# Interleaved attention layers on one core: local scores and values as two tasks each, the band tile kept in SBUF and loaded as rectangles, new orders

## The chip, the cores and the metric

One core of one Trainium2 chip runs the whole program in one launch. The metric is the device time of an execution in microseconds (us). A core has five engines with queues of their own: TensorE (PE; its weight loads are listed as PEld), VectorE (DVE), ScalarE (ACT), GpSimd (POOL) and SyncE (SP), which issues nearly all DMA transfers here. Each engine works its queue off in order.

## The reference

Four layers follow each other, of kinds A, B, A, B, each on the layer norm of its input, with a residual sum. Sequence 2048, width 512, 32 heads of 16, float32.

```python
def _A_ref(x, wqkv, wo):                 # dilated window: 8 keys, 2 apart
    W, dil = 8, 2
    idx = pos[:, None] - off[None, :]    # off = arange(W) * dil
    logits = einsum("bhsd,bhswd->bhsw", q, kg) * Dh ** -0.5   # kg, vg: k, v at idx
    attn = softmax(where(idx >= 0, logits, -1e9))
    return reshape(einsum("bhsw,bhswd->bhsd", attn, vg)) @ wo

def _B_ref(x, wqkv, wo):                 # the last 256 keys
    mask = (i - j >= 0) & (i - j < 256)
    p = softmax(where(mask, einsum("bhqd,bhkd->bhqk", q, k) * Dh ** -0.5, -1e9))
    return reshape(einsum("bhqk,bhkd->bhqd", p, v)) @ wo

x = A_x
for f, w in ((_A_ref, A), (_B_ref, B), (_A_ref, A), (_B_ref, B)):
    x = x + f(_layernorm(x), *w)
```

## The kernel before

The sequence is cut into 8 chunks of 256 positions. For each pair of layers (A, B) and each chunk, `layer_a` and then `layer_b` add their steps as tasks to a planner, 16 such pairs in all. A task has an engine, an estimated duration, the values that it reads and writes, and a place. The places stand in the table `ORDER`, one number for each task: each engine's queue is sorted by them, so that the table alone fixes the order on an engine. `Plan.order` then plays the queues through with its estimates, and thereby chooses PSUM banks and the sequence in which the instructions are written.

The projections (`proj_t`, lines 1013 to 1015, and `proj_n`, lines 1033 to 1036) are large matmuls of 256 or 512 columns in three float16 products. The rest of TensorE's work are small matmuls on parts of the array. In layer A, a chunk is split into even and odd positions, t = 0 and 1, of 128 positions each:

- `scores` (line 1159), 64 matmuls for each t, gives each block of 32 queries its 39 keys (`WIN`); a trip through DRAM (`shelve`, `band`) picks the 8 of each query; then comes the softmax.
- The softmax's weights are written into `bands`. `put` (line 1244) stores them in a zeroed DRAM buffer `ptd` with a stride that shifts each query's 8 weights to the right place among 39 keys, and `get` (line 1250) loads the result as the band tile `pt`: 39 partitions (keys), for 2 x 16 pairs of queries and 32 heads, in two transfers, one for each half of the partitions. `window` (line 1239) loads the values `vs` of the same keys.
- `mix` (line 1267), 64 matmuls for each t, multiplies the two; `pick` follows on VectorE, then `finish` with the output projection.

The float32 matmuls of `scores`, `mix` and of the values of layer B run as two passes each, so a task of 64 matmuls is 256 instructions of TensorE with its weight loads. The pool of `pt` has one buffer, so the second `get` of a chunk waits for the first `mix`.

In layer B, line 1377 (q) computes scores for the row maxima, which VectorE takes (lines 1396 and 1392); lines 1528 and 1583 are the scores and values themselves, between them ScalarE's exponentials (1538, 1550) and masks on GpSimd or VectorE (1567, 1561). Its queries and keys come as stk<-re (line 1319), the row maxima through md (1428, 1434). Line 1709 are matmuls on nothing that keep TensorE busy early in the program; there are 110 such tasks.

Of the kernel before, what the change touches and what calls it, by code (L numbers as in the profile page):

```python
# [11 lines left out]
F32 = mybir.dt.float32  # L12
# [6 lines left out]
P = 128  # L19
# [415 lines left out]
SLOW = 0.25  # L435
LEAVE = {"Q": 0.13, "C": 0.185, "X": 0.15, "V": 0.17, "R": 0.13, "F": 0.105, "": 0.0}
AGAIN = {"PE": 0.0, "DVE": 0.11, "ACT": 0.12, "POOL": 0.055, "SP": 0.0}
RECENT, WARM, EDGE = 3.4, 0.31, 0.05


class Buf:
# [206 lines left out]
def kernel(  # L648
# [276 lines left out]
    def norm(l, c):  # L925
# [31 lines left out]
        for t in range(2):  # L957
            if layers[l] == "A" and (l, c) != (0, 0):
# [8 lines left out]
                def low(xn=xn):  # L967
                    return xn.t.bitcast(F16)[:, 0:D]
# [780 lines left out]
```

## Time and profile before

| | |
|---|---|
| time, median of 3 runs | 1544.56 us (1534.9 to 1547.74) |
| the profiled execution | 1535.14 us, span of its instructions 1533.4 us |
| mean granted TensorE clock | 0.937 |
| TensorE busy | 1352.3 us |
| VectorE, ScalarE, GpSimd busy | 869.0, 829.8, 386.9 us |
| DMA | 203.06 MB, mean 132 GB/s |

Busy time is the time in which an engine has an instruction under way, and small matmuls run beside each other. Idle time is listed with what ended it: "issue" is a wait for nothing that the profile shows. A profile line such as "L1267 <- DMA pt<-ptd" reads: the instruction of line 1267 waited for the transfer from `ptd` to `pt`.

### The profile page before, as it was taken

The page shows a single profiled execution, that of the slowest core. Times are in us where ns is not written, and L with a number is a line of the kernel's source. Part 1 is how long each engine was busy: PE and PEld are TensorE (multiplying, and loading weights), DVE is VectorE, ACT ScalarE, POOL GpSimd, SP SyncE. Part 2 cuts the span into 40 slices and gives each one's busy share as a digit, 9 for nine tenths or more (in the row PEclk, how much of TensorE's full clock was granted, in tenths as well). Part 3 has the DMA queues.
Part 4 walks back from the last instruction along what each step waited for, and adds up shares of the span by engine and source line. Part 5 has one row for each costly group of instructions (what it writes and reads, how often), then busy time and mean ns, then how long its engine had stood idle before and what let it go on. Part 6 is the DMA issues. An engine that isn't in the chain of part 4 may idle for free.

```text
span 1533.4 us, 64202 instructions
## 1 busy us (share of the span) xinstructions
PE 1352.3 (88%) x28126; PEld 870.6 (57%) x28126; DVE 869.0 (57%) x1966; ACT 829.8 (54%) x1301; POOL 386.9 (25%) x828
## 2 busy tenths in 40 slices
PE   8989989898898988979889897989989899897876
PEld 7665657465464745646456463755647375564643
DVE  5635664754636455455663617466562755646486
ACT  8634647465654655636555373647657355453633
POOL 3410202222213323213132031315033311231231
PEclk9999999889999999999899898999999999898988
DMA  9874463645537255553445647365464646536222
GB/s 252 217 170 138 129 129 109 152 118 150 120 108 168 81 166 112 143 143 106 113 98 167 129 133 162 85 171 127 140 123 125 149 101 155 121 105 158 81 80 58
DMA packets 183377, 203.06 MB, mean 132 GB/s; under 512 B 92188, under 2 KB 122652, under 8 KB 183096
## 3 DMA queue, kind: packets, MB, share of 16 engines
q1 hardware_dynamic: 182840, 198.69, 51.2%
q8 instruction: 220, 3.60, 1.0%
q14 instruction: 61, 0.50, 0.1%
q10 hardware_dynamic: 256, 0.26, 0.1%
HBM read 101.97 MB, written 79.36 MB: 118 GB/s over the span
## 4 chain that ended last, share of the span: by engine, by line
PE 55%; DMA 16%; DVE 10%; issue 7%; SPq 7%; ACT 5%; POOL 1%; DVEq 0%; ACTq 0%; POOLq 0%
PE banks L1583 7%; PE banks L1013 7%; PE banks L1014 6%; PE banks L1015 6%; PE banks L1033 4%; PE banks L1035 4%; DMA pt<-ptd 4%; PE banks L1377 4%; PE banks L1036 4%; PE banks L1528 4%; PE banks L1267 3%; DVE m L1392 3%; PE banks L1159 2%; DMA sd<-s 2%; SPq L1308 2%
## 5 line engine op out<-in xcount | busy, mean ns | idle before, releaser
L1392 DVE TENSOR_REDUCE m<-banks 128x2 f32<-128x512 f32 x448 | 302.6, 689 | 9.0
L1538 ACT ACTIVATE p<-banks,sclB 128x896 f32<-128x896 f32 x224 | 221.3, 1006 | 77.4 <-PE banks L1528 62.1
L1396 DVE COPY_PREDICATED banks<-trm,banks 128x128 f32<-128x128 int16 x448 | 125.4, 291 | 150.6 <-PE banks L1377 142.6
L1377 PE MATMUL banks<-stk,stk 48*64 48x192 f16 (+3 forms) x3584 | 147.8, 249 | 49.1 <-DMA stk<-re 15.7
L1567 POOL TENSOR_SCALAR_AFFINE_SELECT p<-p 64x256 f32<-64x256 f32 x296 | 116.7, 416 | 271.4 <-ACT p L1538 258.9
L1567 POOL TENSOR_SCALAR_AFFINE_SELECT ps<-ps 64x256 f32<-64x256 f32 x272 | 109.3, 423 | 255.9 <-ACT ps L1550 251.1
L1377 PEld LDWEIGHTS <-stk 48*64 48x64 f16 x3584 | 83.0, 111 | 141.8 <-issue 117.3
L1528 PE MATMUL banks<-stk,stk 64*64 64x128 f16 (+3 forms) x3584 | 126.8, 245 | 22.8 <-ACT p L1538 7.7
L1583 PE MATMUL banks<-p,v 64*32 64x192 f32 (+1 forms) x3584 | 129.9, 386 | 9.6 <-issue 6.0
L1550 ACT ACTIVATE ps<-banks,sclB 128x768 f32<-128x768 f32 x112 | 100.1, 899 | 50.5 <-PE banks L1528 36.1
L1528 PEld LDWEIGHTS <-stk 64*64 64x64 f16 x3584 | 71.8, 110 | 84.6 <-issue 73.0
L1167 ACT COPY s<-banks 128x624 f32<-128x624 f32 x64 | 74.5, 1263 | 60.2 <-DMA sd<-s 32.6
L1298 DVE SCALAR_TENSOR_TENSOR el<-banks,eh 128x512 f16<-128x512 f32 x64 | 42.8, 688 | 106.0 <-ACT eh L1295 79.8
L1267 PE MATMUL banks<-pt,vs 39*32 39x64 f32 x4096 | 63.1, 252 | 37.9 <-DMA pt<-ptd 18.4
L1583 PEld LDWEIGHTS banks<-p,v 64*32 64x32 f32 x3584 | 68.6, 113 | 46.7 <-issue 24.0
L1600 ACT COPY os<-banks 128x256 f32<-128x256 f32 x112 | 41.3, 373 | 95.7 <-PE banks L1583 91.1
L1597 DVE TENSOR_TENSOR os<-os,banks 128x256 f32<-128x256 f32 x104 | 42.7, 418 | 87.9 <-ACT os L1600 79.8
L1583 PE MATMUL banks<-ps,v 64*32 64x64 f32 (+1 forms) x3584 | 77.0, 260 | 12.2 <-issue 12.1
L1583 PEld LDWEIGHTS banks<-ps,v 64*32 64x32 f32 x3584 | 69.1, 112 | 22.5 <-issue 18.4
L1267 PEld LDWEIGHTS banks<-pt,vs 39*32 39x32 f32 x4096 | 52.5, 114 | 51.3 <-issue 33.2
L1014 PE MATMUL banks<-xl,wA0h 128*128 128x256 f16 x256 | 71.9, 281 | 1.7 <-issue 1.7
L1013 PE MATMUL banks<-xh,wA1h 128*128 128x256 f16 x256 | 70.8, 277 | 2.7 <-DMA xh<-ht 2.7
(214 smaller groups left out, 3107.4 us busy)
## 6 DMA issues: line engine op xcount, KB each, us to landing
stk<-re SPq DMA_DIRECT2D x256, 96.0 KB
sd<-s SPq DMA_DIRECT2D x128, 156.0 KB
pt<-ptd SPq DMA_DIRECT2D x64, 312.0 KB
re<-eh SPq DMA_DIRECT2D x128, 128.0 KB
vs<-vd SPq DMA_DIRECT2D x64, 156.0 KB
vd<-ve SPq DMA_DIRECT2D x32, 256.0 KB
xm<-y SPq DMA_DIRECT2D x32, 256.0 KB
re<-el SPq DMA_DIRECT2D x64, 128.0 KB
```

The source lines that it names most:

```text
L1013: nc.tensor.matmul(ps[mp].t[:, i], wh, xh, start=k == 0, stop=False)
L1014: nc.tensor.matmul(ps[mp].t[:, i], wh, xl, start=False, stop=False)
L1015: nc.tensor.matmul(ps[mp].t[:, i], wl, xh, start=False, stop=k == 3)
L1267: nc.tensor.matmul(acc.t[32 * r : 32 * r + 32, bb].rearrange("p (a x q u) -> p a x q u", a=2, q=16, u=2)[:, :, 2 * m + b2], vs.t[k, b2, 32 ...
L1377: nc.tensor.matmul(o, lhs, k, start=True, stop=True, tile_position=(64 * par, 64 * h))
L1392: nc.vector.tensor_reduce(out=m.t[:, :, u, qb], in_=ps.t[:, :, 0 : 2 * P], op=ALU.max, axis=AX.X)
L1396: nc.vector.copy_predicated(t[:, :, 0:64], trm[:, 0].bitcast(I16).unsqueeze(1).broadcast_to([P, 2, 64]), t[:, :, C : C + 64])
L1528: nc.tensor.matmul(ps.t[64 * h : 64 * h + 64, par, at + x0 : at + x0 + q1 - q0], stk[hf, kt][r, col, k0 : k0 + 64], stk[hf, 0][r, col, q0: ...
L1538: nc.scalar.activation(big.t[:, 2 * i : 2 * i + 2], ps.t[:, :, 0:448], AF.Exp, scale=scl["B", 1])
L1550: nc.scalar.activation(small.t.rearrange("p (i m) x -> p m i x", i=2), ps.t[:, :, 0:384].rearrange("p m (i x) -> p m i x", i=2), AF.Exp, s ...
L1567: E.affine_select(out=v, in_=v, pattern=[[0, 4], [a, 64]], compare_op=op, fill=0.0, base=0, channel_multiplier=-a)
L1583: nc.tensor.matmul(acc.t[32 * mm : 32 * mm + 32, h, q0:q1], vv[r, blk, 17 * hd : 17 * hd + 32], x.t[r, mm, x0 : x0 + q1 - q0], start=begin ...
```

## The change

1. The band tile becomes one constant tile `ptt`, zeroed once on GpSimd. `get` loads, for each half of the partitions, two rectangles in place of the whole: for the first 8 pairs of queries the first 23 keys, for the last 8 pairs the last 23 keys. What lies outside stays zero. There are four transfers of 23 partitions for each `get` in place of two of 39.
2. `scores` and `mix` become two tasks each, of half the matmuls, so that other work can stand between the halves.
3. The planner has a new term: TensorE's instructions are fetched at `FETCH` each us into a store of `STORE`, each task says how many it takes (`rec`), and a task can't be shorter than its instructions take to come.
4. Some estimates change: size 1350 of `get` becomes 700, its time on SyncE 0.8 becomes 1.65; sizes of `clear`, the transposes and `shelve`, and the time of the masks on GpSimd grow.
5. The table `ORDER` is new throughout, one list for each scope.

```diff
 ORDER = {
-    "S": [16, 13, 12, 0, 11, 7, 6, 35, 19],
+    "S": [13, 21, 3, 19, 0, 2, 7, 20, 21, 13],
...
+FETCH, STORE = 67.0, 160.0
...
-                us /= clock
+                store = min(STORE, store + FETCH * (now - seen))
+                us = max(us / clock, (t.rec - store) / FETCH)
+                store = min(STORE, store + FETCH * us - t.rec)
+                seen = now + us
...
+    ptt = cst.tile([P, 2, 16, H, 2], F32, name="ptt")
+    vptt = Val()
...
+    plan.add("POOL", 1.8, lambda: nc.gpsimd.memset(ptt, 0.0), w=[vptt])
...
-            def scores(t=t, pbs=pbs):
-                for m in range(4):
+            def scores(m0, t=t, pbs=pbs):
+                for m in range(m0, m0 + 2):
...
-            plan.add("PE", 1.5, scores, r=[*vq, *vk, vhalo], w=vpb, mode="X", act=0.7)
+            for m0 in (0, 2):
+                plan.add("PE", 0.75, lambda f=scores, m0=m0: f(m0), r=[*vq, *vk, vhalo], w=vpb, mode="X", act=0.35, rec=128)
...
-            def get(t=t, pt=pt):
+            def get(t=t):
                 x = ptd[t]
                 for bb in range(2):
-                    nc.sync.dma_start(pt.t[64 * bb : 64 * bb + WIN].rearrange("p a q s u -> p a (q s u)"),
-                                      bass.AP(tensor=x.tensor, offset=x.offset + 2 * bb * 65 * H * 32, ap=[[64 * H, WIN], [65 * H * 32, 2], [1, 32 * H]]))
+                    for e in range(2):
+                        nc.sync.dma_start(ptt[64 * bb + 16 * e : 64 * bb + 16 * e + WIN - 16, :, 8 * e : 8 * e + 8].rearrange("p a q s u -> p a (q s u)"),
+                                          bass.AP(tensor=x.tensor, offset=x.offset + (2 * bb * 65 * 32 + 16 * e * 65) * H, ap=[[64 * H, WIN - 16], [65 * H * 32, 2], [1, 16 * H]]))
...
-            plan.add("SP", 0.8, get, r=[vptd[t]], w=[vpt], size=1350)
+            plan.add("SP", 1.65, get, r=[vptd[t]], w=[vptt], size=700)
...
-            def mix(acc=acc, vs=vs, pt=pt):
-                for m in range(4):
+            def mix(m0, acc=acc, vs=vs):
+                for m in range(m0, m0 + 2):
...
-            plan.add("PE", 2.0, mix, r=[vvs, vpt], w=[va], mode="V", act=1.2)
+            for m0 in (0, 2):
+                plan.add("PE", 0.85, lambda f=mix, m0=m0: f(m0), r=[vvs, vptt], w=[va], mode="V", act=0.5, rec=128)
```

Lines of the changed program lie 12 to 14 further down than before (`mix` at 1280, `scores` at 1171, `get` at 1263). Three places of the order:

SyncE, chunk 4 of the first pair of layers, from the first `get` to past the second (md, stk: layer B's row maxima, queries and keys; xl, xh, y, x: inputs; vs: local values). Before:

```order
L1250 DMA pt_4_0_6424<-ptd_148 39x2x1024 x2
L978 DMA_TRANSPOSE xl_5_6390<-xn_5_0_5363 128x4x128
L1428 DMA md_3_0_6453<-mt_3_0_6427 4x32x32 x2
L977 DMA_TRANSPOSE xh_5_6325<-ht_5_0_5385 128x4x128
L1099 DMA y_4_0_6505<-in_A_x_dram 128x512
L1434 DMA stk_0_132<-md_3_0_6453 2x1024 x2
L1250 DMA pt_4_1_6600<-ptd_149 39x2x1024 x2
L1428 DMA md_3_1_6612<-mt_3_1_6510 4x32x32 x2
```

And now:

```order
L1263 DMA ptt<-ptd_146 23x2x512 x4
L1442 DMA md_3_0_6492<-mt_3_0_6465 4x32x32 x2
L1333 DMA stk_2_134<-re_3_1_5640 48x1x1024 x2
L1256 DMA ptd_147<-bands 64x9x64
L1448 DMA stk_0_129<-md_3_0_6492 2x1024 x2
L1251 DMA vs_4_1_6636<-vd_1_149 39x2x512 x2
L1263 DMA ptt<-ptd_147 23x2x512 x4
L1442 DMA md_3_1_6727<-mt_3_1_6704 4x32x32 x2
```

Each `get` is four transfers with 23 rows in place of two with 39, and other transfers stand behind it.

TensorE, the `mix` of chunk 4 in the second pair of layers, t = 0. Before, behind layer B's values:

```order
L1583 MATMUL banks<-ps_3_1_19846,v_140 32x64
L1583 MATMUL banks<-ps_3_1_19846,v_138 32x64
L1267 MATMUL banks<-pt_4_0_19861,vs_4_0_19622 32x2x32 x64
L1013 LDWEIGHTS wA0h
L1013 MATMUL banks<-xh_5_19885,wA0h 128x256
L1014 LDWEIGHTS wA0h
```

And now:

```order
L1391 LDWEIGHTS stk_0_132
L1391 MATMUL banks<-stk_2_134,stk_0_132 64x128
L1280 MATMUL banks<-ptt,vs_4_0_19498 32x2x32 x64
L1025 LDWEIGHTS wA0h
L1025 MATMUL banks<-xh_5_19761,wA0h 128x256
L1026 LDWEIGHTS wA0h
```

The values of layer B have gone from in front of the `mix`; its two halves still follow each other, as one row of 64.

TensorE, the two `scores` of the first chunk. Before they are one run:

```order
L1709 LDWEIGHTS idf
L1709 MATMUL banks<-idf 128x256
L1159 MATMUL banks<-k_0_270,qm_0_483 64x39 x128
L1013 LDWEIGHTS wA1h
L1013 MATMUL banks<-xh_1_456,wA1h 128x256
```

And now the first of them, the second coming some 80 rows later:

```order
L862 MATMUL banks<-idf,axA_540 2x128
L1171 MATMUL banks<-k_0_489,qm_0_474 64x39 x64
L881 MATMUL banks<-a1A_588,ones 128x4
L1723 LDWEIGHTS idf
L1723 MATMUL banks<-idf 128x256
```

The run of 128 matmuls has become two of 64.

More of the change, by code (lines that the diff above doesn't have):

```diff
@@ L497 @@
 class Task:
-    __slots__ = ("eng", "us", "fn", "n", "after", "bufs", "mode", "start", "end", "size", "act", "place", "ready", "scope", "alt")
+    __slots__ = ("eng", "us", "fn", "n", "after", "bufs", "mode", "start", "end", "size", "act", "place", "ready", "scope", "alt", "rec")
 class Plan:
@@ L507, in begin, with add @@
         self.scope, self.k = scope, 0
-    def add(self, eng, us, fn, r=(), w=(), mode="", size=0, act=0.0, alt=None):
+    def add(self, eng, us, fn, r=(), w=(), mode="", size=0, act=0.0, alt=None, rec=5):
         t = Task()
-        t.eng, t.us, t.fn, t.mode, t.size, t.act, t.scope = eng, us, fn, mode, size, act, self.scope
+        t.eng, t.us, t.fn, t.mode, t.size, t.act, t.scope, t.rec = eng, us, fn, mode, size, act, self.scope, rec
         t.place, t.alt = ORDER[self.scope][self.k] if self.scope in ORDER else len(self.tasks), alt
@@ L556, in order @@
         dma, mode, tail, use, since = 0.0, "", "", 0.0, 0.0
+        store, seen = STORE, 0.0
         out = []
@@ L673 @@
     cst = ctx.enter_context(tc.tile_pool(name="cst", bufs=1))
-    for name, bufs in (("px", 4), ("pqm", 1), ("pk", 1), ("psc", 1), ("pl", 1), ("ppt", 1), ("pvs", 1), ("pve", 1), ("po4", 1), ("pos", 2), ("pxn", 2),
+    for name, bufs in (("px", 4), ("pqm", 1), ("pk", 1), ("psc", 1), ("pl", 1), ("pvs", 1), ("pve", 1), ("po4", 1), ("pos", 2), ("pxn", 2),
                        ("pxt", 2), ("pp6", 2), ("pp7", 2), ("pqk", 2), ("poh", 2), ("ps1", 1), ("psm", 2)):
@@ L771 @@
     for i in range(2):
-        plan.add("SP", 1.5, lambda i=i: clear(i), r=[vbands], w=[vptd[i], vvd[0, i, -1], vvd[2, i, -1]], size=1100)
+        plan.add("SP", 1.5, lambda i=i: clear(i), r=[vbands], w=[vptd[i], vvd[0, i, -1], vvd[2, i, -1]], size=1500)
     wt, vwt, psc, pscs, scl, vscl = {}, {}, {}, {}, {}, {}
@@ L976, in norm @@
                 plan.add("POOL", 1.12, rest, r=[vxn, vht], w=[vlt], mode="S", alt=("DVE", 0.6))
-                plan.add("SP", 1.24, lambda sl=sl, ht=ht: nc.sync.dma_start_transpose(xh.t[:, :, sl], ht.t), r=[vht], w=[vh], size=16)
-                plan.add("SP", 1.24, lambda sl=sl, low=low: nc.sync.dma_start_transpose(xl.t[:, :, sl], low()), r=[vlt], w=[vl], size=16)
+                plan.add("SP", 1.28, lambda sl=sl, ht=ht: nc.sync.dma_start_transpose(xh.t[:, :, sl], ht.t), r=[vht], w=[vh], size=200)
+                plan.add("SP", 1.28, lambda sl=sl, low=low: nc.sync.dma_start_transpose(xl.t[:, :, sl], low()), r=[vlt], w=[vl], size=200)
                 continue
@@ L1181, in band @@
                                   bass.AP(tensor=x.tensor, offset=x.offset, ap=[[2 * (WIN + 1) * H, 64], [(WIN + 1) * H, 2], [1, W * H]]))
-            plan.add("SP", 1.9, shelve, r=vS, w=[vsd], size=450)
+            plan.add("SP", 1.9, shelve, r=vS, w=[vsd], size=600)
             plan.add("SP", 0.4, band, r=[vsd], w=[vL[t]], size=160)
@@ L1232, in layer_a @@
             vs = buf("pvs", [P, 2, D], F32, "vs", f"vs{l}_{c}_{t}")
-            pt = buf("ppt", [P, 2, 16, H, 2], F32, "pt", f"pt{l}_{c}_{t}")
-            vvs, vpt = Val(vs), Val(pt)
+            vvs = Val(vs)
             def window(t=t, vs=vs):
@@ L1267, in mix @@
                                 nc.tensor.matmul(acc.t[32 * r : 32 * r + 32, bb].rearrange("p (a x q u) -> p a x q u", a=2, q=16, u=2)[:, :, 2 * m + b2],
-                                                 vs.t[k, b2, 32 * (4 * m + r) : 32 * (4 * m + r) + 32], pt.t[k, :, :, 16 * b2 + 4 * m + r],
+                                                 vs.t[k, b2, 32 * (4 * m + r) : 32 * (4 * m + r) + 32], ptt[k, :, :, 16 * b2 + 4 * m + r],
                                                  start=True, stop=True, tile_position=(64 * bb, 32 * r))
@@ L1379, in layer_b @@
                     if first:
-                        plan.add("PE", 0.172, scores, r=[vst[hf, 0, hp], vst[hf, now, hp]], w=[vps], mode="R", act=0.14)
+                        plan.add("PE", 0.172, scores, r=[vst[hf, 0, hp], vst[hf, now, hp]], w=[vps], mode="R", act=0.14, rec=8)
                     else:
-                        plan.add("PE", 0.15, halves, r=[vst[hf, 0, hp], vst[hf, now, hp], vst[hf, bef, hp]], w=[vps], mode="Q", act=0.12)
+                        plan.add("PE", 0.15, halves, r=[vst[hf, 0, hp], vst[hf, now, hp], vst[hf, bef, hp]], w=[vps], mode="Q", act=0.12, rec=16)
                     def top(u=u, qb=qb, ps=ps, m=m, x0=x0):
@@ L1476, in expo @@
                                                      AF.Exp, scale=scl["B", 1])
-                            plan.add("PE", 0.172, scores, r=[vst[hf, 0, hp], vst[hf, "m", hp], vst[hf, kt, hp]], w=[vps], mode="R", act=0.14)
+                            plan.add("PE", 0.172, scores, r=[vst[hf, 0, hp], vst[hf, "m", hp], vst[hf, kt, hp]], w=[vps], mode="R", act=0.14, rec=8)
                             plan.add("ACT", 0.8, expo, r=[vps, vscl["B", 1]], w=[vp[i]])
@@ L1503, in layer_b @@
                         nxt = Val(acc)
-                        plan.add("PE", 0.67, values, r=[vp2, *vvt[(c - 1 + b) % 3], *([chain] if chain else [])], w=[vacc, nxt], mode="C", act=0.16)
+                        plan.add("PE", 0.67, values, r=[vp2, *vvt[(c - 1 + b) % 3], *([chain] if chain else [])], w=[vacc, nxt], mode="C", act=0.16, rec=64)
                         chain = nxt
@@ L1538, in expo @@
                         nc.scalar.activation(big.t[:, 2 * i : 2 * i + 2], ps.t[:, :, 0:448], AF.Exp, scale=scl["B", 1])
-                    plan.add("PE", 0.205, lambda f=score, ps=ps, i=i: f(ps, 0, i, wide_), r=need, w=[vps], mode="Q", act=0.165)
+                    plan.add("PE", 0.205, lambda f=score, ps=ps, i=i: f(ps, 0, i, wide_), r=need, w=[vps], mode="Q", act=0.165, rec=16)
                     plan.add("ACT", 0.93, expo, r=[vps, vscl["B", 1]], w=[vbig[i]])
@@ L1551, in expo @@
                                          AF.Exp, scale=scl["B", 1])
-                plan.add("PE", 0.18, thin, r=need, w=[vps], mode="Q", act=0.14)
+                plan.add("PE", 0.18, thin, r=need, w=[vps], mode="Q", act=0.14, rec=32)
                 plan.add("ACT", 0.8, expo, r=[vps, vscl["B", 1]], w=[vsmall])
@@ L1569, in layer_b @@
                 vm2, vs2 = Val(big), Val(small)
-                plan.add("POOL", 1.5, lambda E, f=mask, x=big: f(E, x, 448), r=[*vbig, vtri], w=[vm2], mode="S", alt=("DVE", 0.65))
-                plan.add("POOL", 1.5, lambda E, f=mask, x=small: f(E, x, 192), r=[vsmall, vtri], w=[vs2], mode="S", alt=("DVE", 0.65))
+                plan.add("POOL", 1.65, lambda E, f=mask, x=big: f(E, x, 448), r=[*vbig, vtri], w=[vm2], mode="S", alt=("DVE", 0.65))
+                plan.add("POOL", 1.65, lambda E, f=mask, x=small: f(E, x, 192), r=[vsmall, vtri], w=[vs2], mode="S", alt=("DVE", 0.65))
                 acc = Banks(psum, 2, [P, 2, 512])
@@ L1588, in layer_b @@
                 vals = [*vvt[c % 3], *vvt[(c - 1) % 3]]
-                plan.add("PE", 0.8, lambda f=value, x=big, w=wide2: f(x, w, True), r=[vm2, *vals], w=[vacc, nxt], mode="V", act=0.2)
-                plan.add("PE", 0.36, lambda f=value, x=small, w=thin2: f(x, w, False), r=[vs2, *vals, nxt], w=[vacc], mode="V", act=0.09)
+                plan.add("PE", 0.8, lambda f=value, x=big, w=wide2: f(x, w, True), r=[vm2, *vals], w=[vacc, nxt], mode="V", act=0.2, rec=64)
+                plan.add("PE", 0.36, lambda f=value, x=small, w=thin2: f(x, w, False), r=[vs2, *vals, nxt], w=[vacc], mode="V", act=0.09, rec=64)
                 def some(hp=hp, hq=hq, hf=hf):
```

776 rows, old and new, of the table ORDER are left out of this document.

## The prediction

> **What bounds the kernel now.** I read the head of the page first, then the chain of work that ended last, then the list of TensorE's waits.
>
> ```profile
> PE 1352.3 (88%) x28126; PEld 870.6 (57%) x28126; DVE 869.0 (57%) x1966; ACT 829.8 (54%) x1301; POOL 386.9 (25%) x828
> PE 55%; DMA 16%; DVE 10%; issue 7%; SPq 7%; ACT 5%; POOL 1%; DVEq 0%; ACTq 0%; POOLq 0%
> ```
>
> TensorE is the bound: 1352.3 of 1533.4 us busy, so 181 us idle, and no other engine is near. The rest of the chain is latency, and DMA is its largest part. What ends TensorE's idle time (columns: engine, line, what it waited for, total us, times, longest):
>
> ```profile
> PE banks L1267 <- DMA pt<-ptd: 18.4, 13, 3.4
> PE banks L1583 <- issue: 18.1, 14, 2.8
> PE banks L1159 <- issue: 16.5, 9, 3.9
> PE banks L1377 <- DMA stk<-re: 15.7, 14, 2.5
> PE banks L1377 <- DVE m L1392: 14.7, 28, 2.2
> PE banks L1267 <- issue: 11.1, 9, 1.9
> PE banks L1377 <- issue: 7.9, 5, 2.2
> ```
>
> Two things stand out. Four rows read "issue", 18.1 + 16.5 + 11.1 + 7.9 = 53.6 us, in which TensorE waited for nothing but its own instructions. And the top row is the load of the band tile, `get`, before the products with the local values (`mix`): 13 of the 32 mixes wait for it already, so they stand close behind their loads and any delay of a `get` reaches TensorE.
>
> **The load of the band tile** is what decides. Before, a `get` is two transfers of 39 rows; after, four of 23 rows. First the time of one now, by the longest pieces of the chain (start, us, what; the first and a late one of ten like them), the issue on SyncE, and the sizes:
>
> ```profile
> 100.63 6.26 DMA pt<-ptd
> 1303.83 6.10 DMA pt<-ptd
> ...
> 1189.38 2.69 DMA stk<-re
> ...
> L1250 SPq DMA_DIRECT2D pt<-ptd x64: 298/372/1577, 65.7 to 1409.2; - x64
> ...
> stk<-re SPq DMA_DIRECT2D x256, 96.0 KB
> ...
> pt<-ptd SPq DMA_DIRECT2D x64, 312.0 KB
> ```
>
> The chain enters at the second transfer, so a whole `get` lands 0.37 + 6.2 = 6.6 us after its first issue. The new bytes are 4 x 23 x 2 x 512 x 4 = 377 thousand, against 639 thousand. If bytes were all, each new transfer (92 KB) would land as the 96 KB stk<-re does, 2.7 us after issue, the fourth one 3 x 0.37 later: 3.8 us. That is the lower bound, a gain of 2.8 us for each `get`.
>
> The upper bound comes from how a transfer is spread over the 16 DMA engines. Here is a `get` that has the queues nearly to itself (issued at 1399.59; beside it only four transfers of 4 KB), by short windows; the last two columns are the busy share of the 16 engines and GB/s. The second window row is of loads with rows of 2 KB, stk<-re among them:
>
> ```profile
> 1399.59 0.73 SPq L1250 DMA_DIRECT2D pt<-ptd  x2
> ...
> 1400.50:1401.00 0.50, 0.50 (x4) 0.16 (x2) 0.50 (x2) 0.00 (x0) 0.00 (x0) 1.00 0.79 221
> 1401.00:1402.00 1.00, 1.00 (x19) 0.43 (x18) 0.96 (x4) 0.23 (x1) 0.00 (x0) 1.00 0.85 242
> 1402.00:1403.00 1.00, 0.89 (x18) 0.36 (x10) 1.00 (x4) 0.00 (x0) 0.00 (x0) 1.00 0.84 177
> ```
> ```profile
> 125.00:126.00 1.00, 1.00 (x6) 0.48 (x5) 0.16 (x1) 0.00 (x0) 0.00 (x0) 1.00 0.61 205
> ```
>
> With 39 rows the share stands still at 0.79 to 0.85. 39 = 3 x 13, and 13 of 16 engines is 0.81: each of 13 engines has three rows, and three engines have nothing. Both transfers of the `get` are under way in these windows; had the second taken other engines than the first, all 16 would be busy. So I read two things: rows are dealt out in equal numbers, and always to the same first engines. 23 is prime. Equal numbers leave one engine for all 23 rows, and the same one for all four transfers. An engine moves 242 / (0.85 x 16) = 17.8 GB/s in the window of the `get` and 205 / (0.61 x 16) = 21.0 in that of the 2 KB rows, whose pieces are as long as the new ones. 377 KB then take 18 us (at 21.0) to 21 us (at 17.8). With about 1 us from the issue to the first byte (1399.59 against the window at 1400.50) and half for the end, the new `get` lands 19.5 to 22.5 us after its first issue. Between 3.8 and 22.5 I take **19.5 us**, since the rows speak for equal shares: 12.9 us later than now.
>
> The Trainium skill says the same in "DMA: Bandwidth & Descriptors", section "Queues, rings and completion order": a transfer uses the largest number of engines up to 16 that divides the slowest dimension of both sides, 127 partitions put everything on one, and the lowest-numbered engines are taken. The 0.85 for 39 rows agrees; no run here shows a prime count yet. By that rule the get is on one engine.
>
> **From the load to the time.** Little can hide 12.9 us. The tile has one copy, so the second `get` of a chunk waits for the first `mix` as before, and what TensorE does meanwhile was laid out for loads of 6.6 us. I count 1 us of slack for each (13 of 32 have none): 32 x 11.9 = **+381 us**.
>
> Behind a `get` on SyncE stand, in the new order, md, stk<-re, the next band and vs; their shares on that one engine queue behind 18 us of band rows. SyncE now does this after a `get`:
>
> ```profile
> 676.50 0.80 SPq L1250 DMA_DIRECT2D pt<-ptd  x2
> 677.39 0.34 SPq L1656 DMA_DIRECT2D scr<-rc  x1
> 677.84 0.38 SPq L1099 DMA_DIRECT2D y<-xm  x1
> 683.77 0.54 SPq L1661 DMA_DIRECT2D os<-scr  x1
> ...
> SPq L1661 <- DMA scr<-rc: 12.4, 4, 5.5
> ```
>
> Two more issues and then 5.5 us of nothing, until scr<-rc, 32 KB issued behind the get, has landed. Behind the new get that is some 18 us. As TensorE stands in the same window, I count it within the stall and keep it as a rival.
>
> A stall also costs afterwards. Windows around a wait of 3.4 us (second number after the busy times: the granted TensorE clock):
>
> ```profile
> 680.00:682.00 2.00, 0.00 (x0) 0.00 (x0) 0.58 (x2) 1.45 (x4) 0.00 (x0) 1.00 0.86 212
> 682.00:684.00 2.00, 0.65 (x35) 0.55 (x36) 0.00 (x0) 0.08 (x1) 0.00 (x0) 0.92 0.23 74
> 684.00:686.00 2.00, 2.00 (x133) 1.90 (x125) 0.33 (x1) 0.00 (x0) 0.00 (x0) 0.50 0.48 61
> 686.00:688.00 2.00, 2.00 (x86) 1.82 (x73) 1.06 (x2) 0.59 (x1) 0.00 (x0) 0.73 0.97 267
> ```
>
> The clock falls to 0.50 for some 3.4 us, worth 1.7 us. A part of the gets has this already, so I add 1.2 us each: **+38**. The longer stalls give the other engines time: of the idle time that is neither issue nor pt (181 - 53.6 - 18.4 = 109 us) I take off a good quarter, **-30**.
>
> **Instruction supply.** A burst of small matmuls outruns it:
>
> ```profile
> 732.69 0.59 PE L1583 MATMUL banks<-ps,v 64*32 64x128 f32 x32
> 733.21 1.65 PE L1159 MATMUL banks<-k,qm 32*64 32x39 f32 x120
> 737.09 0.32 PE L1159 MATMUL banks<-k,qm 32*64 32x39 f32 x8 [2.23 <-issue]
> ```
>
> Counted in the two programs' orders, runs of TensorE work without a projection between them hold 9172 instructions beyond the first 256 of their run before, 6328 after (31% fewer); runs of 384 and more fall from 36 to 18. 53.6 us x 0.31 = **-17**. The split itself hardly takes part: all 32 pairs of `mix` halves stay adjacent, and 10 of the 32 score pairs are separated, mostly by 8 to 16 other small matmuls. The Trainium skill ("Runtime: NRT & Kernel Launch", "Instruction fetch mechanics") has fetching mostly hidden; the 2.23 us above is not. If that were right here, the sum would be 17 higher.
>
> **Changes of tiling.** Changes between matmuls of different tiling fall from 1061 to 957, 52 pairs. Their price, by starts:
>
> ```profile
> 714.05 0.27 PE L1014 MATMUL banks<-xl,wB0h 128*128 128x256 f16 x1
> 714.16 0.27 PE L1015 MATMUL banks<-xh,wB0l 128*128 128x256 f16 x1
> 714.36 0.56 PE L1528 MATMUL banks<-stk,stk 64*64 64x256 f16 x24
> ...
> 708.34 0.39 PE L1528 MATMUL banks<-stk,stk 64*64 64x256 f16 x8
> 708.56 0.31 PE L1377 MATMUL banks<-stk,stk 48*64 48x256 f16 x8
> ...
> 719.86 0.39 PE L1528 MATMUL banks<-stk,stk 64*64 64x256 f16 x8
> 720.18 0.28 PE L1013 MATMUL banks<-xh,wA0h 128*128 128x256 f16 x1
> ```
>
> In: 0.20 instead of 0.11. Out: 0.32 instead of 0.22. 52 x 0.19 = **-10**.
>
> **At nothing:** the memset of the tile runs once, on GpSimd, which idles 75% of the span; if something waited for it, it is a few us. 64 more issues are 64 x 0.37 = 24 us of SyncE, inside the stalls above. The planner's costs only choose order and banks. A few masks change engine (82 to 76 on VectorE, 568 to 592 halves on GpSimd): neither is the bound.
>
> **Sum:** 381 + 38 - 30 - 17 - 10 = +362. The profiled execution took 1535.14 us (span 1533.4), so **1897, say 1900 us**. The median of the runs, 1544.56, lies 0.6% above that execution, less than my terms are sure to.
>
> **Rivals.**
> 1. *The rows are spread after all* (12 engines with two rows each): the get lands at 3.8 us. 2.8 us less on 13 waits of 18.4 us in total removes some 15; with -17 and -10, and a quarter given back to other waits, 1535 - 31 = 1504. For it: the bytes. Against it: 0.85 rather than 1.0 for 39 rows. It decides as soon as a transfer of 23 rows uses five engines or more. Chance 0.10; this is the case on the faster side.
> 2. *One engine each, but four different ones:* 94 KB / 21 = 4.5, plus 1.1 and 1.5, 7.1 us, half a us worse: 1535 + 16 - 27 = 1524, no change. Against it: two transfers of 39 rows would then fill 16 engines. Chance 0.06.
> 3. *The queue behind the get stalls too:* what TensorE would do during the load needs transfers that stand behind it, so nothing of the 19.5 us is covered. 32 x 18 = 576 in place of 381, and 1535 + 576 + 38 - 30 - 27 = 2092. For it: SyncE's 5.5 us of nothing above. Against it: work of other chunks has its data already. Chance 0.22.
>
> Forecast 0.62. **Range:** the forecast's own goes from 1640 (a get that lands at 15 us and finds 4.5 us of cover: 32 x 3.9 + 38 - 57 = 106) to 2000 (22.5 us and 1 us: 32 x 14.9 + 38 - 57 = 458); with rival 3 it reaches 2150, and 1640 to 2150 leaves out rivals 1 and 2 and a little more. A measurement of this kernel tells about 1% from no change (its three runs span 0.8%). Faster by over 1%: 0.11 (rival 1 and a part of 2); within 1%: 0.05; slower: 0.84.
>
> **What would show it.** Right: "DMA ptt<-ptd" leads TensorE's waits with 300 us or more, a piece of the chain of some 18 us for each get, DMA share near 0.06 in windows in which a get is alone, more of the clock row at 0.5; issue waits near 37 us. Wrong: pieces of 3 to 7 us, a share of 0.7 or more during a get, and the old list of waits.

## The result, and the profile after

The changed kernel takes **1870.68 us**, median of 4 runs (1863.68 to 1876.81), against 1546.15 us (1534.9 to 1550.21): a ratio of 1.2112, 95% interval [1.2031, 1.2193]. The profiled execution took 1874.45 us; its span is 1872.7 us at a mean granted clock of 0.845.

The head of the page, the largest group of waits and the size of the new transfers:

```profile
PE 1375.1 (73%) x28126; PEld 895.2 (48%) x28126; DVE 863.9 (46%) x1961; ACT 825.9 (44%) x1299; POOL 404.9 (22%) x856
PEclk9868979889797886988869797896978979788788
L1280 PE MATMUL banks<-ptt,vs 39*32 39x64 f32 x4096 | 77.8, 305 | 385.5 <-DMA ptt<-ptd 265.2
ptt<-ptd SPq DMA_DIRECT2D x128, 92.0 KB
```

TensorE idles 1872.7 - 1375.1 = 497.6 us in place of 181.1, and 385.5 of these lie in front of `mix` (line 1280), 37.9 before. In the list of TensorE's waits nearly all of this idle time goes by three names:

```profile
PE banks L1280 <- DMA ptt<-ptd: 265.2, 46, 7.7
PE banks L1280 <- issue: 84.7, 15, 7.7
PE banks L1280 <- DMA vs<-vd: 23.0, 3, 12.2
...
PE banks L1597 <- issue: 4.5, 7, 0.9
...
PE banks L1171 <- issue: 3.4, 5, 1.8
```

The "issue" of line 1280 is mostly the load too: its 15 waits are 5.6 us long on average (1.4 us in the kernel with 39 rows and the same order, below), its longest is the same 7.7 us, and the timeline of TensorE shows one such wait beside three of the other name. These are the mixes of t = 0 and t = 1 of one chunk (start, duration, count, in brackets the idle time ahead):

```profile
1729.85 0.39 PE L1280 MATMUL banks<-ptt,vs 39*32 39x64 f32 x2 [5.63 <-DMA ptt<-ptd]
1737.57 2.01 PE L1280 MATMUL banks<-ptt,vs 39*32 39x64 f32 x125 [7.32 <-DMA ptt<-ptd]
...
1751.63 0.39 PE L1280 MATMUL banks<-ptt,vs 39*32 39x64 f32 x2 [4.71 <-DMA ptt<-ptd]
1759.27 2.01 PE L1280 MATMUL banks<-ptt,vs 39*32 39x64 f32 x125 [7.25 <-issue]
```

A mix stands twice. Its first two matmuls read the lower half of the partitions, which the first two transfers fill; everything after them needs the other two, which are there 7.7 us later (1729.85 to 1737.57). Two transfers, 188 KB, take 7.5 us at the 25 GB/s shown below, so the transfers lie one behind the other. The chain of waits shows both gets of the chunk (start, duration, what; its longest pieces; a piece begins only with the issue of the transfer that it names):

```profile
1720.67 16.76 DMA ptt<-ptd
1737.57 2.01 PE banks L1280 x121
1739.63 0.68 SPq L1251
1741.52 13.65 DMA ptt<-ptd
```

A get, a mix, two issues for `vs`, a get, and the second mix: from 1720.67 to 1761 the end of the chunk waits in line, and of these 40 us the chain holds less than 5 us of matmuls. In the second get it names the third transfer, which lands at 1755.17; the mix starts only at 1759.27, when the fourth has landed. And here is what the 16 DMA engines do in the meantime (the last two columns are busy share and GB/s):

```profile
1744.00:1745.00 1.00, 1.00 (x28) 0.34 (x19) 0.65 (x3) 0.84 (x2) 0.81 (x3) 1.00 0.06 25
1752.00:1754.00 2.00, 0.02 (x1) 0.00 (x0) 0.00 (x0) 0.00 (x0) 0.00 (x0) 0.50 0.06 25
```

0.06 is 1/16: one engine carries the whole load at 25 GB/s, and the clock of TensorE (the number ahead of the share) falls to 0.50 meanwhile. From the first issue to the last landing, by the semaphore updates in the trace, a get takes 17.9 us on average over its 32 occurrences (16.8 to 18.9); before it took 6.7 (5.8 to 8.3).

### The profile page after: what moved, and what is told of

Read it like the earlier page. It is cut to its first block, busy times and chain, and to the rows that moved or that the text cites. A ratio compares the mean times of both kernels' runs of the same rounds, so it can differ in the third digit from the quotient of the medians.

```text
span 1872.7 us, 64356 instructions
## 1 busy us (share of the span) xinstructions
PE 1375.1 (73%) x28126; PEld 895.2 (48%) x28126; DVE 863.9 (46%) x1961; ACT 825.9 (44%) x1299; POOL 404.9 (22%) x856
## 5 line engine op out<-in xcount | busy, mean ns | idle before, releaser
L1280 PE MATMUL banks<-ptt,vs 39*32 39x64 f32 x4096 | 77.8, 305 | 385.5 <-DMA ptt<-ptd 265.2
L1280 PEld LDWEIGHTS banks<-ptt,vs 39*32 39x32 f32 x4096 | 63.7, 143 | 394.5 <-issue 367.7
L1079 ACT CAST oh<-banks 128x512 f16<-128x512 f32 x32 | 18.8, 587 | 415.4 <-DVE banks L1285 415.4
L1581 POOL TENSOR_SCALAR_AFFINE_SELECT p<-p 64x256 f32<-64x256 f32 x300 | 122.7, 431 | 347.0 <-ACT p L1552 333.1
L1285 DVE COPY_PREDICATED banks<-odd,banks 128x512 f32<-128x512 int16 x32 | 22.3, 696 | 377.1 <-PE banks L1280 377.0
L1581 POOL TENSOR_SCALAR_AFFINE_SELECT ps<-ps 64x256 f32<-64x256 f32 x292 | 115.8, 418 | 359.5 <-ACT ps L1564 354.4
L1391 PE MATMUL banks<-stk,stk 48*64 48x128 f16 (+3 forms) x3584 | 145.0, 253 | 45.6 <-DMA stk<-re 21.7
L1542 PE MATMUL banks<-stk,stk 64*64 64x192 f16 (+3 forms) x3584 | 124.4, 250 | 22.2 <-DVE m L1406 6.2
L1597 PE MATMUL banks<-p,v 64*32 64x256 f32 (+1 forms) x3584 | 131.5, 399 | 3.6 <-DVE p L1575 1.3
L1180 ACT COPY s<-banks 128x624 f32<-128x624 f32 x64 | 74.5, 1263 | 66.0 <-DMA sd<-s 42.9
L1683 POOL TENSOR_TENSOR oc<-oc,os 128x512 f32<-128x512 f32 x23 | 29.5, 1292 | 245.0 <-DMA os<-scr 75.1
```

The lines of the kernel that those rows point to most:

```text
L1180: nc.scalar.copy(S_.t.rearrange("p k (s r) -> p r s k", r=4)[:, 2 * i : 2 * i + 2], pbs[i].t[:, :, 0 : 8 * WIN].rearrange("p r (s k) -> p ...
L1280: nc.tensor.matmul(acc.t[32 * r : 32 * r + 32, bb].rearrange("p (a x q u) -> p a x q u", a=2, q=16, u=2)[:, :, 2 * m + b2], vs.t[k, b2, 32 ...
L1391: nc.tensor.matmul(o, lhs, k, start=True, stop=True, tile_position=(64 * par, 64 * h))
L1542: nc.tensor.matmul(ps.t[64 * h : 64 * h + 64, par, at + x0 : at + x0 + q1 - q0], stk[hf, kt][r, col, k0 : k0 + 64], stk[hf, 0][r, col, q0: ...
L1581: E.affine_select(out=v, in_=v, pattern=[[0, 4], [a, 64]], compare_op=op, fill=0.0, base=0, channel_multiplier=-a)
L1597: nc.tensor.matmul(acc.t[32 * mm : 32 * mm + 32, h, q0:q1], vv[r, blk, 17 * hd : 17 * hd + 32], x.t[r, mm, x0 : x0 + q1 - q0], start=begin ...
```

## The experiments

Theory: 23 is prime, rows are dealt to engines in equal numbers, so one engine moves all four rectangles. Rivals: the count of transfers, the shorter pieces or the single tile are slow; or the new order is what stalls. Four kernels cross the size of the get with the order. Lines differ by a few between kernels: `mix` is 1280, 1279, 1271 or 1282 below.

### 24 rows in place of 23

```diff
-                        nc.sync.dma_start(ptt[64 * bb + 16 * e : 64 * bb + 16 * e + WIN - 16, :, 8 * e : 8 * e + 8].rearrange("p a q s u -> p a (q s u)"),
-                                          bass.AP(tensor=x.tensor, offset=x.offset + (2 * bb * 65 * 32 + 16 * e * 65) * H, ap=[[64 * H, WIN - 16], [65 * H * 32, 2], [1, 16 * H]]))
+                        nc.sync.dma_start(ptt[64 * bb + 16 * e : 64 * bb + 16 * e + 24, :, 8 * e : 8 * e + 8].rearrange("p a q s u -> p a (q s u)"),
+                                          bass.AP(tensor=x.tensor, offset=x.offset + (2 * bb * 65 * 32 + 16 * e * 65) * H, ap=[[64 * H, 24], [65 * H * 32, 2], [1, 16 * H]]))
```

> The changed kernel with rectangles of 24 rows in place of 23 (the 24th row is zero in the buffer); nothing else differs. Theory (equal numbers of rows on an engine: 23 is prime, so one engine; 24 = 12 x 2, so twelve): each get lands some 4 us after its first issue, the waits for it fall from 265 us by name (385 us at the line of mix) to under 25 us, and the time is near 1505 us, between 1490 and 1530, where rival 1 of the prediction had put it. Rival (the delay comes from the number of transfers, the shorter pieces or the single tile): nothing changes, 1860 to 1880 us, and the share of the 16 DMA engines stays at 0.06 while a get is alone.

Measured: **1471.07 us** (1470.99 to 1474.53), ratio to before 0.9573 [0.9517, 0.9628]. One row more in each rectangle, 4% more bytes, and the program is 400 us shorter and 4.3% faster than the kernel before. Page, and three windows around a get:

```profile
PE 1322.8 (90%) x28126; PEld 865.6 (59%) x28126; DVE 865.9 (59%) x1961; ACT 825.5 (56%) x1299; POOL 405.3 (28%) x856
L1280 PE MATMUL banks<-ptt,vs 39*32 39x64 f32 x4096 | 59.8, 240 | 26.6 <-issue 13.5 <-DMA ptt<-ptd 10.2 <-DVE m L1406 2.0
```
```profile
1354.60:1355.10 0.50, 0.42 (x28) 0.39 (x27) 0.00 (x0) 0.00 (x0) 0.00 (x0) 1.00 0.79 258
1355.10:1355.60 0.50, 0.50 (x24) 0.26 (x10) 0.00 (x0) 0.29 (x1) 0.00 (x0) 1.00 0.70 250
1355.60:1356.10 0.50, 0.50 (x8) 0.09 (x9) 0.39 (x1) 0.50 (x2) 0.00 (x0) 1.00 0.72 143
```

The idle time in front of `mix` is 26.6 us, the share 0.70 to 0.72 where 12/16 is 0.75 (0.79 in the half us before, with a `vs` of 39 rows issued just ahead of the get), and the get lands after 5.0 us. The rivals that blame count, pieces or tile are out: all three are the same here. But the time lies 34 us under what I had expected.

### The old order with 23 rows, and with 24

The constant tile and the four rectangles put into the kernel before; its order and its undivided tasks stay. The diff of the get is that of the change (23) and the one above (24).

> The kernel before, its order and undivided tasks, with only the get changed: four rectangles of 23 rows into the constant tile. Theory (the get alone carries the loss, and 32 stalls of about 12 us come of it whatever the order): 1546 + 324 + 27 = 1897 us, between 1850 and 1940, with the wait for the get at 300 us or more. Rival (the new order makes the loss larger, since it puts md and stk<-re behind the get and brings mix closer): 1700 to 1800 us.

Measured: **1871.68 us** (1870.67 to 1874.52), ratio 1.2175 [1.2105, 1.2246]. Page and waits:

```profile
PE 1398.0 (75%) x28126; PEld 898.0 (48%) x28126; DVE 869.8 (46%) x1966; ACT 829.3 (44%) x1301; POOL 388.3 (21%) x829
...
L1271 PE MATMUL banks<-ptt,vs 39*32 39x64 f32 x4096 | 78.0, 305 | 354.7 <-DMA ptt<-ptd 203.6
```
```profile
PE banks L1271 <- DMA vs<-vd: 82.9, 9, 11.7
```

The get alone carries the whole loss, whatever the order. What stands behind it shows in the last row: in nine of the 16 chunks the old order issues the values `vs` of the second mix behind the second get, and in eight of these the mix waits for them (issued at 502.69, behind the get of 491.38, they hold it up until 510.64).

> The kernel before, its order and undivided tasks, with four rectangles of 24 rows into the constant tile. Theory: the get lands some 2.5 us sooner than two transfers of 39 rows; it had 18 us of waits by name, so at most that and the clock lost behind it can go: 1525 to 1540 us. Rival (the get's bytes and packets compete with other transfers, so less traffic helps the whole program): under 1515 us. Rival (four issues on SyncE cost what the shorter load gains): 1541 to 1555 us.

Measured: **1505.55 us** (1502.23 to 1514.97), ratio 0.9801 [0.9737, 0.9866], so 35 us less than the 1540.16 us of before, measured beside it: more than the theory gave, and under the bound of the rival that less traffic helps.

### The new order with the old get

```diff
-                    for e in range(2):
...
+                    nc.sync.dma_start(ptt[64 * bb : 64 * bb + WIN].rearrange("p a q s u -> p a (q s u)"),
+                                      bass.AP(tensor=x.tensor, offset=x.offset + 2 * bb * 65 * H * 32, ap=[[64 * H, WIN], [65 * H * 32, 2], [1, 32 * H]]))
```

> The changed kernel with the get of before: two transfers of 39 rows, into the constant tile; new orders, divided tasks and planner's rules are kept. By the prediction's terms for supply (-17) and changes of tiling (-10) it takes 1508 to 1520 us, the waits named issue at TensorE's lines are near 37 us, and the wait for the get is near the 18 us of before. Rival (the new order itself stalls, since it was laid out for a shorter get, or since other transfers stand behind the get): 1560 us or more, with the get or md, stk<-re in front of TensorE.

Measured: **1512.68 us** (1509.65 to 1515.29), ratio 0.9843 [0.9776, 0.9911]: 27.5 us less than before. Page and waits:

```profile
PE 1340.1 (89%) x28126; PEld 875.1 (58%) x28126; DVE 866.6 (57%) x1961; ACT 825.1 (55%) x1299; POOL 406.2 (27%) x856
```
```profile
PE banks L1279 <- DMA ptt<-ptd: 24.4, 20, 1.9
...
PE banks L1279 <- issue: 17.9, 13, 3.6
...
PE banks L1596 <- issue: 9.2, 11, 1.9
...
PE banks L1171 <- issue: 5.2, 6, 1.7
```

With other lines the issue waits sum to 36.5 us (59.4 before, over all lines), near the 37 expected, and TensorE is busy 12.2 us less. The order does not stall.

So with 39 rows the new order gains 27.5 us, with 24 rows 34.5 (1505.55 against 1471.07), and with 23 rows 1. There TensorE is 22.9 us less busy but idles 24.9 us more, since the new order covers 0.9 us less of each get (17.85 us less 385.5/32 is 5.8 covered, against 17.8 less 354.7/32, 6.7).

### 25 rows

> The changed kernel with rectangles of 25 rows. Theory (equal numbers of rows: 25 = 5 x 5, so five engines with 82 KB each for a get, in place of one with 377 KB or twelve with 33 KB): 82 KB at 25 GB/s (the rate of the one engine with 23 rows) are 3.3 us, at the 15 GB/s of twelve engines 5.5 us, so with 2.8 us of issues and latency the get lands after 6 to 8 us; it took 6.8 us with two transfers of 39 rows, so the time is near that kernel's 1513 us, between 1495 and 1545. Rival (23 rows are slow because the number is odd or not a multiple of 8, and not because of the count of engines): 1800 us or more. Rival (only one row count is slow, and the rest fills all engines): 1471 to 1480 us.

Measured: **1496.65 us** (1489.08 to 1504.11), ratio 0.9734 [0.9677, 0.9791]; the get lands after 6.5 us. Two windows of a get behind which only two transfers of 8 KB were issued until 387.11, and its wait:

```profile
386.00:387.00 1.00, 1.00 (x25) 0.49 (x12) 0.96 (x3) 0.44 (x1) 0.00 (x0) 1.00 0.33 125
387.00:388.00 1.00, 1.00 (x13) 0.39 (x11) 1.00 (x4) 0.08 (x1) 0.00 (x0) 1.00 0.32 123
```
```profile
PE banks L1280 <- DMA ptt<-ptd: 25.0, 24, 1.8
```

0.32 is 5/16, at 5 x 25 GB/s. An odd count that isn't prime is in between, as its largest divisor up to 16 says. With 39 rows, 25, 24 and 23 the shares are 0.85, 0.32, 0.70 to 0.72 and 0.06, against 13/16, 5/16, 12/16 and 1/16. The rule of the Trainium skill ("DMA: Bandwidth & Descriptors", section "Why a DMA increments its semaphore by 16 and not by 1", where the rule stands, and not in the section that the prediction names) that a transfer runs on the largest number of engines, at most 16, that divides its slowest dimension on both sides agrees with all four. A second count does not depend on what else is on its way: in the trace the DMA side raises the semaphore of each of these transfers 14, 6, 13 and 2 times, once more than 13, 5, 12 and 1 engines.

The get lands only 0.3 us sooner than two transfers of 39 rows do (6.5 against 6.8 us), and yet the program is some 16 us shorter (the two were measured apart, and their intervals just overlap). This points to the bytes, 410 in place of 639 thousand, without showing it.

### Two of the four rectangles with 23 rows

```diff
                     for e in range(2):
+                        n = 23 + e
```

`n` takes the place of the two `WIN - 16`, the number of rows.

> Of the four rectangles of a get, the first of each half has 23 rows and the second 24. Theory (each 23-row transfer sits on one engine, both on the same, 94 KB each at 25 GB/s, so 7.5 us in place of 15.1, and 2.8 us of issues and latency): the get lands after 10 to 11 us; 5.9 us of it were covered with 23 rows everywhere, so TensorE idles some 4.6 us for each get, 32 x 4.6 = 147 us at the line of mix against 24 with 24 rows, and 20 to 30 us more in lower clock: 1471 + 123 + 25 = 1619, between 1570 and 1660. Rival (the two 23-row transfers go to different engines and run side by side): the get lands after 6.6 us and the time is 1490 to 1510. Rival (any prime transfer holds up all that follow on the queue in full): over 1750.

Measured (`mix` is line 1281 here): **1644.84 us** (1639.85 to 1649.03), ratio 1.0732 [1.0675, 1.0790]; the get lands after 10.9 us (10.1 to 12.9). TensorE's timeline at one mix, the group of `mix`, and windows around this stall:

```profile
1505.26 0.27 PE L1281 MATMUL banks<-ptt,vs 39*32 39x64 f32 x2 [0.65 <-DVE banks L1411]
1509.51 2.01 PE L1281 MATMUL banks<-ptt,vs 39*32 39x64 f32 x125 [3.99 <-DMA ptt<-ptd]
```
```profile
L1281 PE MATMUL banks<-ptt,vs 39*32 39x64 f32 x4096 | 74.8, 300 | 167.0 <-DMA ptt<-ptd 142.7
```
```profile
1506.00:1508.00 2.00, 0.00 (x0) 0.00 (x0) 0.47 (x2) 0.00 (x0) 0.00 (x0) 1.00 0.40 149
1508.00:1510.00 2.00, 0.49 (x36) 0.52 (x39) 0.00 (x0) 0.00 (x0) 0.00 (x0) 0.55 0.07 18
1510.00:1512.00 2.00, 2.00 (x126) 1.83 (x117) 0.42 (x1) 0.00 (x0) 0.00 (x0) 0.50 0.12 29
1512.00:1514.00 2.00, 2.00 (x56) 1.03 (x48) 1.68 (x4) 0.90 (x2) 0.00 (x0) 0.50 0.40 128
```

Both 23-row transfers are on one engine, one after the other. Of each get some 5.7 us are covered (10.9 less 167.0/32 = 5.2), 5.8 with 23 rows everywhere, 5.1 with 39: what TensorE has to do during a get hardly depends on how long the get is. I was 26 us too low: 20 at the stall (167.0 for 147) and some 20 at the clock, less what other waits gave back. TensorE is busy 1368.6 us here, 46 us more than with 24 rows; the full delay, with two waits for each get, mostly 4 to 5 and 7 us, costs 52. The windows show one case of each: here the clock stays at 0.50 until about 1515, 5.5 us after the wait of 4 us has ended (1509.51). In the changed kernel it does so until 1764, 4.7 us after the wait of 7.25 us (1759.27):

```profile
1762.00:1764.00 2.00, 2.00 (x72) 1.55 (x55) 0.73 (x2) 0.58 (x1) 1.71 (x2) 0.50 0.01 4
1764.00:1766.00 2.00, 2.00 (x21) 0.90 (x10) 0.75 (x1) 1.58 (x3) 0.00 (x0) 0.98 0.04 8
```

So in these two kernels the price hardly grows with the length of the stall.

### The saved bytes moved again

One transfer behind each get of the kernel with 24 rows, to a spare buffer that nobody reads; compared with that kernel once more, measured beside it.

```diff
+                nc.sync.dma_start(spare, x[32:64, 0 : 60 * H])
```

> The kernel with 24 rows once more, to compare the others of this call on one chip: 1471 us, between 1465 and 1480, and 4.3% less than before.

> As the kernel with 24 rows, with one more transfer behind each get: 32 rows of 7.7 KB, 246 KB, from the same buffer to a spare one in DRAM, for which nobody waits. So the bytes that the smaller rectangles had saved are moved again, behind the get. Theory (the 24 rows gain by landing sooner, not by their bytes): 1471 to 1480 us, of which some us are the issue. Rival (fewer bytes free the DMA engines for what stands behind the get, and this is half of the gain of 35 to 41 us): 1488 us or more, with stk<-re, md and vs in front of TensorE.

Measured: 1474.01 us (1466.77 to 1479.32), ratio 0.9585 [0.9542, 0.9628], without it; **1489.14 us** (1483.09 to 1499.03), ratio 0.9688 [0.9638, 0.9737], with it. 15 us, and the two intervals don't meet, if only just: my theory that the bytes are worth nothing does not hold. Waits for layer B's queries and keys, without and with it:

```profile
PE banks L1391 <- DMA stk<-re: 20.9, 19, 3.3
```
```profile
PE banks L1393 <- DMA stk<-re: 28.4, 25, 4.0
```

With 25 rows this is the second sign of the same size. Going from 39 rows to 24, 41.6 us in the new order, I read as some 15 us for the bytes and the rest for landing 1.8 us sooner; that split is not shown. The 15 still hold the cost of 32 issues on SyncE, which wasn't measured apart, and the copy writes to DRAM, where the saved bytes went to SBUF.

### Undivided tasks

```diff
-                for m in range(m0, m0 + 2):
+                for m in (range(4) if m0 == 0 else ()):
```

The edit stands in `scores` and in `mix`.

> As the kernel with 24 rows, but scores and mix undivided: the first task of each pair does all 64 matmuls, the second none. All 32 mix pairs are adjacent anyway, and 10 of 32 score pairs become one run of 128 again. Theory (the split hardly takes part): within 6 us of the kernel with 24 rows, and the waits named issue at the line of scores grow by at most 5 us. Rival (the split is what shortens the long runs, so that instructions come in time): 10 to 25 us slower, with the waits named issue back near the 50 us of the old order.

Measured: 1479.00 us (1472.30 to 1487.81), ratio 0.9622 [0.9575, 0.9668], against 0.9585 [0.9542, 0.9628] divided. 5 us, with overlapping intervals; issue waits at `scores` 3.2 against 2.5 us, in all 31.7 against 26.6. The split may gain a little; it doesn't explain the 27 to 35 us of the new order.

## Why the prediction was right, step by step

Each term beside what the profiles show (us):

| term | predicted | measured | from |
|---|---|---|---|
| get, first issue to landing | 19.5 | 17.9 | 32 gets |
| stall at `mix` | +381 | +348 | 385.5 - 37.9 |
| clock | +38 | +35 | busy 1375.1 against 1340.1, same order with 39 rows |
| relief and supply | -30 - 17 | -31 | idle elsewhere: 497.6 - 181.1 - 348 |
| tiling (whatever the order does to busy time) | -10 | -12 | 1340.1 - 1352.3 |
| sum | +362 | +339 | spans, 1872.7 - 1533.4 |

By the medians the change is +324.5 us (1870.68 - 1546.15): the profiled execution of the kernel before, from which the prediction counted, was 11 us under its median. The mechanism was right; that the sum came so near is in part luck. The get's growth was 1.7 us too large (54 us over 32 gets), the slack 0.7 us too large (22 us the other way), and 16 us too much were taken off for relief and supply.

- **One engine for four prime transfers:** shown, by the share of 0.06 and by 24, 25 and twice 23 rows. The size was 1.6 us too large: the engine moves 25 GB/s alone, and I had taken 21.0 from a window in which ten engines worked beside each other. 377 KB are 15.1 us; issues, first byte and end add 2.8, where I had 1.5 (the half us for the end came from no row).
- **Little hides it:** the get grew by 17.9 - 6.7 = 11.2 us, the idle time by 348/32 = 10.9. Slack was 0.3 us, not 1. (The 13 waits that I took for 13 mixes lie in front of 11: two of them wait twice.)
- **Clock:** the 35 us are a difference of busy times at a mean clock of 0.845 against 0.938. TensorE has the same matmuls in the same order in both; that the clock makes up the whole difference is inferred.
- **Supply:** outside `mix` the issue waits fell from 59.4 - 11.1 = 48 to 95.9 - 84.7 = 11 us, more than the 17 I gave; but idle time elsewhere fell by 31 in all, so my separate 30 for relief counted mostly the same microseconds.
- **Marks:** "DMA ptt<-ptd" leads with 265, under the 300 named, since most of the 84.7 us of "issue" at `mix` are the same wait; for that reason the issue waits stand at 95.9 us and not near 37. The chain's pieces are 13 to 17 us, not 18, as they begin with the issue of the transfer named, and the chain reaches back only to 1224 us, so it shows 8 gets of 32. The share came as said, and the clock is lower (0.845 against 0.937), though no slice of its row is down to 0.5.
- **Rival 3** (nothing covered, 2092): 5.8 us of each get are covered, as 5.5 were before (6.7 less 37.9/32), so it didn't come. Its mechanism is there, though: the 82.9 us for `vs` with the old order.
- **Rival 1's price** was wrong. Spread over 12 engines the program takes 1471, not 1504. Its 27 us for order and tiling were right (27.5 alone); for the get I counted only the 15 us of waits that bear its name, and it was worth 35 with the old order and 42 with the new. The name of a wait isn't its worth: bytes that leave the queue (some 15 us, with the limits named above) and a higher clock (busy 1340.1 down to 1322.8) stand under other names.

## What to carry to other kernels

Before a transfer is made smaller, look at the factors of its row count: 23 rows took 17.9 us, 24 rows 5.0, and one zero row more was worth 400 us. The busy share of the DMA engines, in a window where a transfer is nearly alone, tells how many of them carry it (0.06, 0.32, 0.72, 0.85 here). When a load stands close before its reader already, count nearly all of its delay for each repetition (10.9 of 11.2 us here), and 1.4 to 1.6 us of lower clock with it (46 and 52 us for 32 gets).

## What the hardware showed that I had not expected

While one engine works off a backlog, the issues of other transfers on SyncE take long themselves. SyncE's timeline around the second get above:

```profile
1740.78 5.02 SPq L1263 DMA_DIRECT2D ptt<-ptd  x4
1745.90 1.69 SPq L1675 DMA_DIRECT2D os<-scr  x1
1747.63 6.05 SPq L1442 DMA_DIRECT2D md<-mt  x2
1753.73 3.06 SPq L1111 DMA_DIRECT2D y<-xd  x1
```

A get with 25 rows, and md behind it:

```profile
384.16 1.53 SPq L1263 DMA_DIRECT2D ptt<-ptd  x4
385.78 1.28 SPq L1442 DMA_DIRECT2D md<-mt  x2
```

In the whole program 102 issues take more than 2 us each, 343 us together, against 9 and 21 us before and 12 and 26 us with 24 rows; with 23 rows in the old order it is 89 and 316 us, with two of four rectangles at 23 rows 40 and 99. The prediction had 24 us for 64 more issues. What holds an issue back inside the chip no run here shows; that it goes with the one busy engine is shown by these counts: it grows with the number of 23-row transfers and is absent with 24 rows.
